# Local and pooled attention into a split-precision feed-forward: the pooled product halved over both row groups, two more units sent through DRAM, a new table of due times, and larger stores at the end

## The chip, the cores and the metric

One core of one Trainium2 chip. The time is the device time of one launch, in microseconds (us). A core has five engines with a program each: PE (matrix products, 128 x 128 cells that read weights from up to 128 partitions and can be used as smaller tiles), DVE (elementwise, reductions, 32 x 32 transposes), ACT (activations and copies), POOL (elementwise, slower) and SP (here it only issues transfers). ACT issues some transfers too. "64\*64" before a shape is the tile of PE that an instruction uses, rows by columns.

## The reference, cut to what matters

```python
# q, k, v: [8 batches, 8 heads, 576, 64]
def sm_attn(qq, kk, vv):                      # softmax(qq kk^T / 8) vv
    ...
q_d, k_d, v_d = (x.reshape(B, H, 144, 4, D).mean(axis=3) for x in (q, k, v))
out_up = np.repeat(sm_attn(q_d, k_d, v_d), 4, axis=2)      # pooled attention
mask = np.abs(pos[:, None] - pos[None, :]) < 4             # banded attention
out_local = softmax(where(mask, q k^T / 8, -1e9)) v
x = (out_up + out_local) as [4608 tokens, 512]
h = x @ w_in                                  # 512 -> 2048
g = h * np.clip(h + 3.0, 0.0, 6.0) / 6.0
out = g @ w_out                               # 2048 -> 512
```

## The kernel before, in words

**Feed-forward.** The 4608 tokens are nine chunks of 512. For each chunk and each of 16 blocks f of 128 hidden columns, `gemm1` (L1031) makes h in a PSUM bank (tiles h0, h1), ACT makes the clip (L1037), DVE the gate (L1041), ACT the rounded copy gh (L1045, `hi`), DVE or POOL the remainder gl (L1049, `lo`), and `gemm2` (L1081) adds the block into the chunk's four output banks o0 to o3. Every operand is such a pair of a rounded part and a remainder, so that each product takes three matmuls: 12 matmuls of 128 x 512 for a `gemm1`, 12 for its `gemm2`, 3456 in all. The weights are split into such pairs on the chip during the first chunk (`plan_weights`).

**Attention.** A unit is two heads of one batch: 32 units, four per batch, and chunk 0 needs the four units of batch 0, chunk 1 those of batch 1, and so on. A unit has pooled scores (a softmax over 144), banded scores (windows of 64 rows, ten of them in two halves), and two products with V. There are two kinds of units:

- *alone* (before: batches 0 and 1): each step stands by itself in PE's program. Pooled scores `scores_d` L504, mask and banded scores L699 and L707, pooled weights transposed by PE (`trans_d` L597), their product (`pv_d` L678), banded weights transposed by PE (`trans` L732), their product (`pv` L750). For V's last rows PE also does a small sum (`sum_pe` L466).
- *in bursts* (before: batches 2 to 7): weights are written to DRAM by SP (`put_d`, `put`: L610, L637), read back in another arrangement (`get_d`, `get`) and turned by DVE (`turn_d`, `turn_l`). `plan_burst` puts the scores of a new unit and the products of an older one side by side in one piece of PE's program: pooled scores (`scores_d4` L521), banded product (`pv` L750), pooled product (`pv_d4` L666), banded scores (L707). The burst holds the two banks h0 and h1 until DVE has read the results (`mean` L682 on ACT, `mean_too` L685 and `add` L755 on DVE).

In `pv_d4` the 144 pooled keys lie as three groups: group 0 on partitions 0 to 63, group 1 on 64 to 127, and group 2 (32 rows: the last 16 keys once for each of the unit's two heads) on partitions 0 to 63 with zeros filled up to 64 rows, so that products of 64 rows serve for it too.

**Order.** A planner (`Plan`) takes all operations with their dependencies, a cost each, and due times, and writes a fixed program for every engine: `start_of(n)` gives a chunk's start from `T0` and `TC`, `FIRST` the due times of batch 0, `PEN` and `COST` choose between engines for an operation that several can do. Queues are in order: an instruction that waits holds what stands behind it on its engine.

**The end.** The last chunk's output tiles are copied out of PSUM in two halves, ACT then DVE (L996, L998), and stored by SP and ACT, one transfer for each run of at most 36 rows (`stores`, L1002).

## Time and profile before

| what | value |
|---|---|
| time, median of 3 runs | 919.96 us (918.54 to 920.59) |
| the profiled execution | 915.05 us, its span 913.2 us |
| PE busy | 899.2 us, 98% of the span |
| DVE, ACT, POOL busy | 530.9, 430.1, 230.2 us |
| DMA read and written | 69.53 MB, 22.61 MB |
| chain that ended last | PE 91%, DVE 3%, DMA 2%, ACT 1% |

The profiled execution lies below all three of the timed runs (4.91 us under their median), so a sum that is made in its trace is carried to the median as a difference. In the rows of the trace a line starts with the start and the duration in us; "xN" is the count of records. Instructions on PE overlap: the next one's start minus this one's start is the time that PE spent on it. One float32 matmul on a 64-row tile leaves two records.

### The profile page before, as it was taken

How to read it: one execution, taken by the hardware profiler on the slowest of the kernel's cores; microseconds unless marked ns; L12 is line 12 of the kernel's file. 1: busy time of each engine (PE TensorE's matmuls, PEld its weight loads, DVE VectorE, ACT ScalarE, POOL GpSimd, SP SyncE). 2: the span in 40 equal slices, each digit the busy share in tenths (PEclk: the TensorE clock that was granted, in tenths of full speed). 3: DMA queues.
4: the chain of work that ended last, by engine and by line, in shares of the span. 5: the costliest groups of instructions: out<-in, count | busy, mean ns of one | idle time of the engine just before them, and what ended most of it. 6: DMA issues, size and time to landing. Idle time of an engine off the chain costs nothing.

```text
span 913.2 us, 19160 instructions
## 1 busy us (share of the span) xinstructions
PE 899.2 (98%) x7002; PEld 730.9 (80%) x7002; DVE 530.9 (58%) x965; ACT 430.1 (47%) x1438; POOL 230.2 (25%) x316
## 2 busy tenths in 40 slices
PE   8899999999999999999999999999999999999997
PEld 6577778788888888888888888888888888888886
DVE  7989866676755567556745675556654432233222
ACT  5977745566554555345535564455542222222221
POOL 5685532222322231223212330225000000010000
PEclk9999999999999999999999999999999999999999
DMA  9989433666736456355644555555522010001001
GB/s 251 290 231 293 100 82 77 128 120 134 146 85 128 100 112 144 78 104 106 139 97 93 114 116 126 105 104 105 134 59 48 1 47 1 1 1 46 1 1 46
DMA packets 311565, 93.41 MB, mean 102 GB/s; under 512 B 250800, under 2 KB 296880, under 8 KB 311472
## 3 DMA queue, kind: packets, MB, share of 16 engines
q1 hardware_dynamic: 310800, 91.29, 44.4%
q8 instruction: 55, 0.90, 0.4%
q10 hardware_dynamic: 672, 0.91, 0.3%
q14 instruction: 38, 0.31, 0.1%
HBM read 69.53 MB, written 22.61 MB: 101 GB/s over the span
## 4 chain that ended last, share of the span: by engine, by line
PE 91%; DVE 3%; DMA 2%; ACT 1%; SPq 1%; issue 1%; POOL 0%; ACTq 0%; DVEq 0%
PE h L1031 42%; PE o L1081 41%; PE a L707 2%; PE h L750 1%; PE h L666 1%; PE a L521 1%; DMA arena<-in_k_dram 1%; ACT arena L571 1%; DMA out_dram<-arena 0%; DMA pd<-arena 0%; PE a L504 0%; PE a L678 0%; SPq L985 0%; DMA arena<-in_v_dram 0%; PE a L750 0%
## 5 line engine op out<-in xcount | busy, mean ns | idle before, releaser
L1081 PE MATMUL o<-wp,rounded 128*128 128x512 f32 x1728 | 414.4, 392 | 0.0
L1031 PE MATMUL h<-rounded,wp 128*128 128x512 f32 x1728 | 407.8, 391 | 2.0 <-DVE first L755 1.4
L1031 PEld LDWEIGHTS h<-rounded,wp 128*128 128x128 f32 x1728 | 322.6, 188 | 72.0 <-issue 2.8
L1081 PEld LDWEIGHTS o<-wp,rounded 128*128 128x128 f32 x1728 | 321.2, 188 | 69.4 <-issue 0.8
L1041 DVE SCALAR_TENSOR_TENSOR arena<-arena,h 128x512 f32<-128x512 f32 x144 | 97.8, 679 | 127.1 <-ACT arena L1037 126.8
L1037 ACT ACTIVATE arena<-h 128x512 f32<-128x512 f32 x144 | 85.7, 595 | 181.7 <-PE h L1031 180.8
L1045 ACT CAST rounded<-arena 128x512 fp32r<-128x512 f32 x144 | 88.8, 617 | 112.1 <-DVE arena L1041 61.9
L1049 DVE TENSOR_TENSOR rounded<-arena,rounded 128x512 fp32r<-128x512 f32 x105 | 72.4, 692 | 101.5 <-PE o L1081 96.6
L1049 POOL TENSOR_TENSOR rounded<-arena,rounded 128x512 fp32r<-128x512 f32 x39 | 51.9, 1333 | 168.5 <-PE o L1081 88.7
L377 DVE STREAM_TRANSPOSE arena<-arena 128x576 f32<-128x576 f32 x56 | 43.3, 775 | 67.3 <-DMA arena<-in_q_dram 34.1
L571 ACT ACTIVATE arena<-arena 128x64 f32<-128x64 f32 x240 | 80.1, 336 | 0.2
L571 ACT ACTIVATION_READ_ACCUMULATOR arena<-arena 128x1 f32 x240 | 45.3, 189 | 0.0
L453 POOL TENSOR_TENSOR arena<-arena 32x256 f32<-32x256 f32 (+1 forms) x26 | 19.4, 746 | 94.4 <-DMA arena<-in_v_dram 90.7
L547 ACT ACTIVATE arena<-arena 128x1 f32<-128x1 f32 (+1 forms) x78 | 15.0, 192 | 47.6 <-DVE arena L560 47.6
L454 POOL TENSOR_TENSOR arena<-arena 32x128 f32<-32x128 f32 (+1 forms) x26 | 12.8, 494 | 96.9 <-PE h L666 95.7
L682 ACT ACTIVATE arena<-h 128x144 f32<-128x144 f32 x24 | 7.0, 290 | 63.7 <-PE h L666 63.7
L451 DVE TENSOR_REDUCE arena<-arena 128x128 f32<-128x512 f32 (+1 forms) x26 | 27.6, 1061 | 13.4 <-PE h L666 9.2
L934 POOL TENSOR_TENSOR rounded<-arena,rounded 128x768 fp32r<-128x768 f32 (+3 forms) x5 | 8.9, 1789 | 98.4 <-ACT rounded L119 94.8
L415 POOL TENSOR_TENSOR arena<-arena 128x144 f32<-128x144 f32 x52 | 31.8, 612 | 4.1
L588 DVE TENSOR_TENSOR arena<-arena 128x432 f32<-128x432 f32 (+1 forms) x42 | 29.8, 710 | 1.4
L633 DVE STREAM_TRANSPOSE arena<-arena 128x384 f32<-128x384 f32 (+1 forms) x48 | 22.2, 467 | 13.5 <-DMA arena<-pd 13.0
L707 PE MATMUL a<-arena 64*64 64x64 f32 x1160 | 28.7, 224 | 0.0
(192 smaller groups left out, 783.9 us busy)
## 6 DMA issues: line engine op xcount, KB each, us to landing
arena<-in_v_dram SPq DMA_DIRECT2D x58, 160.0 KB
rawp<-in_w_in_dram SPq DMA_DIRECT2D x16, 512.0 KB
rawp<-in_w_out_dram SPq DMA_DIRECT2D x16, 512.0 KB
arena<-in_q_dram SPq DMA_DIRECT2D x112, 72.0 KB
arena<-in_k_dram SPq DMA_DIRECT2D x112, 72.0 KB
pl<-arena SPq DMA_DIRECT2D x24, 320.0 KB
arena<-pl SPq DMA_DIRECT2D x96, 80.0 KB
arena<-in_v_dram SPq DMA_DIRECT2D x28, 256.0 KB
```

Of the source, the lines that this page charges most:

```text
L377: nc.vector.transpose(out=qk[kind], in_=qk[kind])
L415: eng.tensor_tensor(t, t, x[:, :, r], op=ALU.add)
L451: eng.tensor_reduce(out=vd, in_=raw.rearrange("p r e -> p e r"), op=ALU.add, axis=AX.X)
L571: nc.scalar.activation(x[:, j], x[:, j], AF.Exp, bias=m[:, j:j + 1], scale=0.125, accum_out=s[:, j:j + 1])
L588: eng.tensor_tensor(x, x, s.unsqueeze(2).broadcast_to(list(x.shape)), op=ALU.mult)
L707: nc.tensor.matmul(st["ps", g][half:half + WIN, jj * D:jj * D + WIN], qk_of("q")[hs, k_first:k_first + WIN], qk_of("k")[hs, k_first:k_firs ...
L1031: nc.tensor.matmul(st["ps"], win[f][:, wt, kk * P:(kk + 1) * P], xs[part][:, kk], start=(kk == 0 and i == 0), stop=(kk == NK - 1 and i == ...
L1037: nc.scalar.activation(st["t"], st["ps"], AF.Relu, bias=3.0)
L1041: nc.vector.scalar_tensor_tensor(out=t, in0=t, scalar=6.0, in1=st["ps"], op0=ALU.min, op1=ALU.mult)
L1045: nc.scalar.copy(st["gh"], st["t"])
L1049: eng.tensor_tensor(st["gl"], st["t"], st["gh"].bitcast(F32), op=ALU.subtract)
L1081: nc.tensor.matmul(otile[n, m], gt[:, ms], wout[f][:, wt], start=(f == 0 and i == 0), stop=(f == NF - 1 and i == 2),)
```

## The change

1. **Pooled product.** Group 2 is split between both row halves: its weights for the first 24 of each 48 queries stand on partitions 0 to 31, those for the other 24 on partitions 64 to 95, and its 32 rows of V on both. Four products of 64 rows by 144 columns (groups 0 and 1) are followed by four of 32 rows by 3 x 24 columns. The loads of V's last rows, `get_d`, `turn_d`, `head` and the pooled sum of V work on those places; the zeros that filled group 2 are no longer written.
2. **Kinds of units.** `ALONE, APART = 6, 8` count units: units 4 and 5 of batch 1 stay alone, units 6 and 7 go "apart": scores by themselves as an alone unit has them, weights through DRAM, both products in one piece (`pv_all`) in no burst.
3. **Due times and costs.** A table `SHIFT` gives each unit its own offset (from -22.4 to 41.8 us), `T0`, `FIRST`, `LAGW`, `KEEP`, `STAY`, `COST` and `PEN` have new values, the rounded copy gh may go to DVE ("ghi"), pairs of blocks start at block 8 of chunk 0 (`PAIR0`), and a new rule (`sooner`) lets an operation wait for another engine that would end it earlier.
4. **The end.** A tile of the last chunk is copied out by one instruction, ACT or DVE in turn, and whole runs of 36 rows go out in one transfer (`put`), in all chunks. The last two blocks' products of its first two tiles are no longer joined.

The core of the diff:

```diff
-            for g in (0, 1, 2):
-                ks = slice(g % 2 * D, (g % 2 + 1) * D)
+            for g in range(2):
+                ks = slice(g * D, (g + 1) * D)
                 for h in range(2):
                     hs = slice(h * D, (h + 1) * D)
                     nc.tensor.matmul(
-                        st["pod"][g % 2][hs]..., st["vd"][ks, g // 2, hs],
-                        used(st["pdt"][ks], h * D, 2 * D) if g < 2 else used(st["pdt"][ks], 6 * D, D),
-                        start=(g < 2), stop=(g > 0), skip_group_check=True)
+                        st["pod"][g][hs]..., st["vd"][ks, 0, hs],
+                        used(st["pdt"][ks], *((3 * h * D, D) if apart else (h * D, 2 * D))), start=True, stop=False, ...)
+            for g in range(2):
+                ks, q = slice(g * D, g * D + NAR), QB // 2
+                x = st["pdt"][ks]
+                for h in range(2):
+                    hs = slice(h * D, (h + 1) * D)
+                    nc.tensor.matmul(
+                        st["pod"][g][hs]...[:, :, g * q:(g + 1) * q], st["vd"][ks, 1, hs],
+                        bass.AP(..., ap=[x.ap[0], [D, 3], [1, q]]), start=False, stop=True, ...)
...
-            unit = plan_unit(..., due - (1 - u) * unit_time(b))
-            if b < ALONE:
+            unit = plan_unit(..., due - (1 - u) * unit_time(b) + SHIFT[NHP * b + 2 * d + u])
+            if NHP * b + 2 * d + u < APART:
...
+        elif apart:
+            a = op("PE", 1.19, pv_all, t + lv + turned_d + sums, take=bks + [ok] + xbs, ...)
...
-            def hi(st=st, key=key):
-                nc.scalar.copy(st["gh"], st["t"])
+            def hi(eng, st=st, key=key):
+                copy_on(eng, st["gh"], st["t"])
...
-            e = [op("ACT", 0.37, partial(ev_half, 0, nc.scalar), [ready], ...)]
-            e.append(op("DVE", 0.37, partial(ev_half, 1, nc.vector), [ready] + e, ...))
+            e = [op("ACT" if m % 2 == 0 else "DVE", (0.60, 0.69)[m % 2], partial(ev_last, ...), [ready], ...)]
...
-T0, TC, TF, LAG = 55.0, 82.0, 5.1, 2
+T0, TC, TF, LAG = 45.8, 82.0, 5.1, 2
-FIRST = 16.0, 8.0
-ALONE = 2
+FIRST = 4.9, 4.6
+ALONE, APART = 6, 8
+SHIFT = [
+    0.0, 0.0, 0.0, 0.0, -19.4, -16.3, -6.5, -14.0,
...
+    "ghi": {"ACT": (0.17, 1 / 1130), "DVE": (0.09, 1 / 1800)},
```

Line numbers shift with the change: `gemm1` L1031 becomes L1047, `gemm2` L1081 L1097, `pv` L750 L760, the band L707 L717, `scores_d4` L521 L522, `scores_d` L504 L505, the pooled product L666 becomes L667 (64 rows) and L676 (32 rows), the store L1002 L988.

PE's program at the first burst that holds a new and an older unit. Before, the end of the older unit's banded product (L750), its pooled product (h is the pair of banks that the burst holds), and the start of the new unit's banded scores (L707):

```order
L750 MATMUL h_2153<-arena 64x61 x2
L666 MATMUL h_2152<-arena 64x144 x2
L666 MATMUL h_2153<-arena 64x144 x2
L666 MATMUL h_2152<-arena 64x144 x2
L707 MATMUL a_2154<-arena 64x64 x2
```

The same place now:

```order
L760 MATMUL h_2157<-arena 64x61 x2
L667 MATMUL h_2156<-arena 64x144 x2
L667 MATMUL h_2157<-arena 64x144 x2
L676 MATMUL h_2156<-arena 64x3x24 x2
L676 MATMUL h_2157<-arena 64x3x24 x2
L717 MATMUL a_2158<-arena 64x64 x2
```

The third pair of products of 64 rows has become two pairs of 32 rows and half as many columns, between neighbours that use tiles of 64 rows.

PE's program in chunk 0, at unit 7, the last of batch 1. Before, its pooled and banded weights are transposed (L597, L732) and multiplied (L678) in pieces between blocks of the feed-forward:

```order
L1031 MATMUL h_1661<-rounded,wp_1376 128x512 x12
L597 MATMUL a_1688<-ident,arena 128x128 x3
L597 MATMUL a_1693<-ident,arena 16x128 x3
L1081 MATMUL o_872<-wp_1494,rounded 128x512 x3
L1081 MATMUL o_891<-wp_1494,rounded 128x512 x3
L1081 MATMUL o_899<-wp_1494,rounded 128x512 x3
L1081 MATMUL o_911<-wp_1494,rounded 128x512 x3
L678 MATMUL a_1717<-first,arena 64x144 x4
L732 MATMUL a_1723<-ident,arena 128x128 x3
L1031 MATMUL h_1731<-rounded,wp_1425 128x512 x12
L732 MATMUL a_1752<-ident,arena 128x128 x2
```

What an apart unit (here unit 6) has in their place: one piece with both products, and then blocks until the next unit's pooled scores (L505):

```order
L760 MATMUL a_1448<-arena 64x57 x2
L760 MATMUL a_1449<-arena 64x61 x2
L667 MATMUL a_1448<-arena 64x144 x2
L667 MATMUL a_1449<-arena 64x144 x2
L676 MATMUL a_1448<-arena 64x3x24 x2
L676 MATMUL a_1449<-arena 64x3x24 x2
L1097 MATMUL o_856<-wp_1355,rounded 128x512 x3
L1097 MATMUL o_870<-wp_1355,rounded 128x512 x3
L1097 MATMUL o_900<-wp_1355,rounded 128x512 x3
L1097 MATMUL o_908<-wp_1355,rounded 128x512 x3
L505 MATMUL a_1512<-arena 64x144 x6
L1047 MATMUL h_1523<-rounded,wp_1287 128x512 x12
```

The four transposing pieces of the unit are gone from PE; its weights pass SP's queue and DVE instead.

PE's program in chunk 1 between the second burst and the third (L521, the first that holds two units). Before:

```order
L1031 MATMUL h_2057<-rounded,wp_862 128x512 x12
L1081 MATMUL o_2090<-wp_726,rounded 128x512 x3
L1081 MATMUL o_1992<-wp_796,rounded 128x512 x3
L1081 MATMUL o_2003<-wp_796,rounded 128x512 x3
L1081 MATMUL o_2008<-wp_796,rounded 128x512 x3
L1081 MATMUL o_2090<-wp_796,rounded 128x512 x3
L1081 MATMUL o_1992<-wp_966,rounded 128x512 x3
L1081 MATMUL o_2003<-wp_966,rounded 128x512 x3
L1081 MATMUL o_2008<-wp_966,rounded 128x512 x3
L1081 MATMUL o_2090<-wp_966,rounded 128x512 x3
L521 MATMUL a_2154<-arena 64x144 x2
```

Now:

```order
L1097 MATMUL o_2039<-wp_805,rounded 128x512 x3
L1097 MATMUL o_1986<-wp_913,rounded 128x512 x3
L1097 MATMUL o_1991<-wp_913,rounded 128x512 x3
L1097 MATMUL o_2001<-wp_913,rounded 128x512 x3
L1097 MATMUL o_2039<-wp_913,rounded 128x512 x3
L1047 MATMUL h_2082<-rounded,wp_850 128x512 x12
L1047 MATMUL h_2112<-rounded,wp_913 128x512 x12
L1097 MATMUL o_1986<-wp_942,rounded 128x512 x3
L1097 MATMUL o_1991<-wp_942,rounded 128x512 x3
L1097 MATMUL o_2001<-wp_942,rounded 128x512 x3
L1097 MATMUL o_2039<-wp_942,rounded 128x512 x3
L522 MATMUL a_2158<-arena 64x144 x2
```

Between the two bursts stand 51 of the feed-forward's matmuls instead of 39. Behind the third burst follow 12 of `gemm2` and then a `gemm1` in both programs.

## The prediction

> **What bounds the kernel now.** I read the page first: the span, PE's busy time and the chain that ended last.

> ```profile
> span 913.2 us, 19160 instructions
> PE 899.2 (98%) x7002; PEld 730.9 (80%) x7002; DVE 530.9 (58%) x965; ACT 430.1 (47%) x1438; POOL 230.2 (25%) x316
> PE 91%; DVE 3%; DMA 2%; ACT 1%; SPq 1%; issue 1%; POOL 0%; ACTq 0%; DVEq 0%
> ```

> PE is idle for 913.2 - 899.2 = 14.0 us. Anything that is to help takes work from PE, or one of these few idle stretches. Most of the work can't move: two blocks of `gemm1` in a row show what 24 of the feed-forward's matmuls take, from the start of one group to the start of the next.

> ```profile
> 156.82 5.60 PE L1031 MATMUL h<-rounded,wp 128*128 128x512 f32 x24
> 162.26 2.20 PE L1081 MATMUL o<-wp,rounded 128*128 128x512 f32 x9
> ```

> 162.26 - 156.82 = 5.44 us, 0.2267 each; 3456 of them are 783.5 us, and no part of the change touches their number. The idle stretches are next, the largest of PE's waits inside the feed-forward and the stretch where PE is emptiest before the feed-forward runs through.

> ```profile
> PE h L1031 <- DVE first L755: 1.4, 2, 1.3
> 20.00:40.00 20.00, 17.68 (x309) 12.25 (x309) 18.85 (x49) 16.74 (x50) 16.07 (x24) 1.00 0.94 266
> ```

> In the first row (total, times, longest) a `gemm1` waited 1.3 us in one place for DVE's `add`. In the window 20 to 40 us (the columns are PE, PEld, DVE, ACT, POOL busy, the granted clock, DMA share and GB/s) DVE is busy 18.85 of 20 us: this start is DVE's, and PE is idle 2.32 us in it. The clock is 1.00, so nothing below depends on it.

> **Units 6 and 7 through DRAM.** An alone unit's price is the distance between the first rows of two units of batch 1, less the feed-forward between them.

> ```profile
> 97.45 0.39 PE L466 MATMUL a<-arena,four 64*16 64x128 f32 x2
> 97.77 0.95 PE L504 MATMUL a<-arena 64*64 64x144 f32 x12
> 98.65 3.02 PE L1081 MATMUL o<-wp,rounded 128*128 128x512 f32 x12
> 101.50 2.88 PE L1031 MATMUL h<-rounded,wp 128*128 128x512 f32 x12
> 104.23 0.45 PE L699 MATMUL a<-maskb,identb 128*128 128x320 bf16 x2
> ...
> 105.34 3.02 PE L1081 MATMUL o<-wp,rounded 128*128 128x512 f32 x12
> ...
> 122.48 0.39 PE L466 MATMUL a<-arena,four 64*16 64x128 f32 x2
> ...
> 692.82 0.81 PE L750 MATMUL h<-arena 64*64 64x60 f32 x40
> ...
> 694.04 1.21 PE L1081 MATMUL o<-wp,rounded 128*128 128x512 f32 x4
> ```

> From 97.45 to 122.48 are 25.03 us with seven blocks of 12 matmuls, 84 x 0.2267 = 19.04; the unit costs PE 5.99. An apart unit keeps the pooled scores (98.65 - 97.77 = 0.88), mask and band (105.34 - 104.23 = 1.11) and has both products in one piece, as the last units have it (694.04 - 692.82 = 1.22). Each of the three pieces interrupts the feed-forward: the 12 matmuls after the pooled scores took 101.50 - 98.65 = 2.85 against 2.72, so 0.13 each. Together 3.60: 2.39 saved per unit, **-4.8** for two. If an interruption costs twice that, it is -4.0; these are the ends. What the two units now send through SP (two stores, twelve gathers) and DVE (two to three turns each, in place of the copies out of PSUM that are dropped) lies beside PE; it is on the path only where chunk 1 waits for unit 7, which is a rival below.

> **The pooled product.** Its price in a full burst, and the prices of a round of 144 columns and of a change of tile:

> ```profile
> 195.16 0.31 PE L521 MATMUL h<-arena 64*64 64x72 f32 x8
> 195.29 0.76 PE L750 MATMUL h<-arena 64*64 64x60 f32 x40
> 195.87 0.54 PE L666 MATMUL h<-arena 64*64 64x144 f32 x9
> ...
> 196.36 0.75 PE L707 MATMUL a<-arena 64*64 64x64 f32 x36
> 197.05 1.19 PE L1081 MATMUL o<-wp,rounded 128*128 128x512 f32 x4
> ...
> 25.43 0.95 PE L504 MATMUL o<-early 64*64 64x144 f32 x12
> 26.31 0.39 PE L466 MATMUL a<-arena,four 64*16 64x128 f32 x2
> ...
> 36.66 0.86 PE L678 MATMUL a<-early 128*64 128x144 f32 x8
> 37.45 0.82 PE L504 MATMUL a<-arena 64*64 64x144 f32 x9
> ```

> Products on different quarters of the array run together, so time goes by rounds. Before, row half 0 has four rounds of 144 columns (two records for each of groups 0 and 2), row half 1 two; the piece takes 196.36 - 195.87 = 0.49 us. L504 has six rounds and ends in a change of tile, 64\*64 to 64\*16: 6r + c = 26.31 - 25.43 = 0.88. L678 has four rounds and two changes, 128\*64 to 16\*64 within it and then to 64\*64: 4r + 2c = 0.79. So r = 0.121 and c = 0.153; four rounds by this are 0.49, as measured. The new product has two rounds of 144 columns (0.24), then products of 72 columns: 195.29 - 195.16 = 0.13 for the same number of records in L521. Its tiles have 32 rows between neighbours with 64, so two changes come in, 0.31, if such a change costs what those in the rows cost. Then the piece is 0.68, +0.19; without that cost it is 0.37, -0.12. In the 22 full bursts that is +4.1 or -2.6. At four single products (two at the end, two of the apart units) a change of tile to the feed-forward follows anyway, so only one is new: +0.04 or -0.12 each. In all **+4.3**, or -3.1 at the other end. I take the first: the change from 128\*64 to 16\*64 in L678 is a change in rows as well, and it is dear. [...]

> **The wait for PSUM at 181 us.** The 1.3 us stand behind the first full burst.

> ```profile
> 176.78 3.02 PE L1081 MATMUL o<-wp,rounded 128*128 128x512 f32 x12
> ...
> 179.13 0.44 ACT L119 COPY arena<-h 64x72 f32<-64x72 f32 x2 [1.56 <-DMA pd<-arena]
> ...
> 179.59 0.31 DVE L685 SCALAR_TENSOR_TENSOR arena<-h,arena 128x144 f32<-128x144 f32 x1 [1.27 <-ACT arena L119]
> ...
> 180.48 0.81 DVE L755 TENSOR_TENSOR first<-h,arena 128x288 f32<-128x288 f32 x2
> ...
> 181.07 1.16 PE L1031 MATMUL h<-rounded,wp 128*128 128x512 f32 x4 [1.28 <-DVE first L755]
> ...
> 198.57 0.81 DVE L755 TENSOR_TENSOR first<-h,arena 128x288 f32<-128x288 f32 x2
> ...
> 199.91 0.39 PE L1031 MATMUL h<-rounded,wp 128*128 128x512 f32 x1
> ```

> ACT's copy out of the burst's bank waits 1.56 us for the store of the former unit's pooled weights, DVE's `mean_too` waits for ACT, the two adds follow, and only then is the bank free for `gemm1`. Now 51 of the feed-forward's matmuls stand between the second burst and the third in place of 39, 12 x 0.2267 = 2.7 us more for that store. The wait goes: **-1.3** (0 at the other end). What is late next is the same path without the store: behind the next burst the adds end at 199.38 and `gemm1` starts at 199.91, so it has 0.53 us to spare.

> **The end.**

> ```profile
> 906.78 1.29 PE L1081 MATMUL o<-wp,rounded 128*128 128x512 f32 x5
> 906.84 1.65 ACTq L1002 DMA_DIRECT2D out_dram<-arena  x4
> ...
> 908.61 0.38 ACT L996 ACTIVATE arena<-o 128x256 f32<-128x256 f32 x1 [1.48 <-DMA out_dram<-arena]
> 909.02 0.42 DVE L998 TENSOR_SCALAR arena<-o 128x256 f32<-128x256 f32 x1 [1.44 <-DMA out_dram<-arena]
> 909.48 0.87 ACTq L1002 DMA_DIRECT2D out_dram<-arena  x2
> ...
> L981 DVE TENSOR_SCALAR arena<-o 128x512 f32<-128x512 f32 x21 | 14.4, 688 | 6.1 <-DMA out_dram<-arena 4.3 <-PE o L1081 1.0 <-DMA pl<-arena 0.7
> ```

> PE is done at 908.07, but ACT issues transfers until 908.5, copies its half, DVE the other until 909.44, and two more issues follow until 910.35; the span ends 2.85 later. Now DVE alone copies the last tile, 0.69 from about 908.1 to 908.8, and one issue (0.87 / 2 = 0.44) on each queue follows: 909.25, and 2.85 behind it 912.1, that is -1.1. SP's last transfer now holds three runs of 36 rows in one, 216 KB for 72 KB, so I give back 0.4: **-0.7** (ends -0.2 and -1.1). The merged stores of the other chunks are behind PE's work and cost nothing; their cover is a whole chunk.

> **Due times, costs, casts.** They add nothing to PE's work. Up to 115 of the 144 rounded copies go from ACT to DVE; DVE, 58% busy, can hold them, and where it can't is a rival. The start stays bounded by DVE: at most PE's idle 2.3 us of the window above can be won, or as much lost with the longer lists on DVE; I take **0**.

> **The sum**: -4.8 + 4.3 - 1.3 - 0.7 = -2.5. The profiled execution, 915.05 us, would become 912.5; it lies 4.9 below the median of the timed runs, to which I carry the difference: 919.96 - 2.5 = **917.5 us**. With the terms' ends (0.8 + 0.5 + 1.3 + 0.5, and the start's 2.3) this case alone runs from 914.5 to 920.8.

> **The rivals.** *A tile of 32 rows costs no change against one of 64.* Then the product gives -3.1 for +4.3: -9.9, 910.1 us. For it speaks that all tiles here are 64 columns wide; against it the 128 to 16 rows above.

> *DVE frees the banks too late (slower).* Each burst but the first leaves 0.53 us. The copies to DVE may stand right in front of `mean_too` and the adds:

> ```profile
> L121 DVE CAST rounded<-arena 128x512 fp32r<-128x512 f32 x1 | 0.4, 386 | 0.0
> ```

> At 0.39 us one such copy is covered; two, 0.77, exceed the slack by 0.24, and PE waits for that at each of 22 bursts: +5.3, so 922.8 us. From a delay of 0.53 + 2.5 / 22 = 0.64 on the change loses. For it: DVE's total rises by some 45 us. Against it: the adds wait for the burst itself, and what stands before them can be worked off while it runs.

> *Unit 7 comes late for chunk 1.* Its products end about 24 matmuls and a half burst (5.4 + 1.1 us) before chunk 1's first `gemm1`; behind them follow mean, `mean_too` and two adds (0.3 + 0.3 + 0.8), the rounded copy and the remainder, which may be POOL's:

> ```profile
> L934 POOL TENSOR_TENSOR rounded<-arena,rounded 128x768 fp32r<-128x768 f32 (+3 forms) x5 | 8.9, 1789 | 98.4 <-ACT rounded L119 94.8
> ```

> With 1.8 for it and 0.7 for the copy (the cast above, 0.39, by its columns) that is 3.9 of 6.5 us. With one more such remainder ahead of it on POOL it is 5.7; it takes two ahead to wait, and then PE stands 1 us: 918.5, inside the range.

> *The reordering does less than the sum*: the wait at 181 us stays or moves to another burst, and the start is 2.3 us longer: -2.5 + 1.3 + 2.3 = +1.1, 921.1 us.

> **How the numbers follow.** A measurement can tell about 0.2% from no change here, 1.84 us: faster is below 918.1, slower above 921.8. The forecast with the change of tile paid has 0.57; since it lies only 0.6 us below that bound, I give 0.33 of it to faster, 0.22 to same and 0.02 to slower. The rival without that cost has 0.29, all faster. DVE's delay has 0.09, all slower, the weaker reordering 0.05, half of it same and half slower. Rounded: faster 0.62, same 0.25, slower 0.13. The range reaches from 909.2, a little below the second case, to 921.0; what lies outside is the lateness on DVE and a part of the second case with a shorter start.

> **What would show it.** In the changed profile: between L667's first record in a burst and L717's main group 0.68 us if the changes are paid, 0.37 if not. Two more units without the transposing rows L598 and L742, and the stretch from chunk 0's start to chunk 1's shorter by about 4.8 us. No wait of `gemm1` for L765 behind the third burst; where PE's waits list L1047 behind L765 many times, DVE's lateness is right. The last issue ends about 1.2 us behind the last matmul, not 2.3. The forecast is wrong if the start, up to the first gate, moves by more than 2.3 us either way, or if the new order opens waits of PE in chunks 0 and 1 where DVE is at 19 of 20 us.

## The result and the profile after

The changed kernel takes **999.49 us** (median of 4 runs, 997.93 to 1001.4), the kernel before 919.25 in the same comparison: ratio **1.0876**, 95% interval 1.0847 to 1.0906. Forecast were 917.5, with a range to 921.0. This is not one of the terms a little off; something the prediction had at zero costs tens of microseconds.

The page of the changed kernel, the lines that answer to those of before (the fourth is the chain that ended last, the last two are groups of instructions: busy time, mean of one, idle time before them):

```profile
span 997.8 us, 19256 instructions
PE 927.6 (93%) x7092; PEld 742.2 (74%) x7092; DVE 584.0 (59%) x1088; ACT 372.6 (37%) x1333; POOL 184.4 (18%) x227
PEclk9999998998999998999999998999899999999997
PE 22%; DMA 2%; SPq 1%; DVE 0%; ACT 0%; issue 0%; DVEq 0%
...
L1047 PE MATMUL h<-rounded,wp 128*128 128x512 f32 x1728 | 423.4, 401 | 34.4 <-DVE arena L1057 26.0
...
L1001 DVE TENSOR_SCALAR arena<-o 128x512 f32<-128x512 f32 x16 | 11.1, 692 | 52.0 <-DMA out_dram<-arena 49.7 <-PE o L1097 1.7 <-issue 0.6
```

PE is idle for 997.8 - 927.6 = 70.2 us, where it was 14.0, and busy 28.4 us longer, with only 90 records more. Most of the second comes from the third line: slices with a granted clock of 0.8 (in tenths, 8) stand where before there were none. The last line gives the first away: in all, DVE stands still for 49.7 us before it copies output tiles out of PSUM, waiting for an earlier tile's store to land.

PE's waits, as total, times, longest:

```profile
PE h L1047 <- DVE arena L1057: 26.0, 7, 6.4
PE o L1097 <- DVE arena L1001: 8.6, 4, 4.1
PE h L1047 <- DVE first L765: 5.9, 2, 2.9
PE h L522 <- DVE arena L1057: 3.6, 4, 1.8
```

Who waits for the stores (total and times), first the changed kernel's L988, then L985 of before:

```profile
DVE arena L1001: 49.7, 12
ACT arena L999: 17.9, 5
```

```profile
DVE arena L981: 4.3, 6
```

One of the places, the end of a chunk with bursts, in the timeline of the changed kernel (start, duration, what; in brackets the idle time before it and who ended it; SPq is SP issuing transfers):

```profile
370.54 8.32 PE L1047 MATMUL h<-rounded,wp 128*128 128x512 f32 x36
...
372.42 3.13 SPq L988 DMA_DIRECT2D out_dram<-arena  x4
...
375.66 6.55 SPq L373 DMA_DIRECT2D arena<-in_q_dram  x4
380.26 0.60 ACT L999 ACTIVATE arena<-o 128x512 f32<-128x512 f32 x1 [5.56 <-DMA out_dram<-arena]
...
383.42 0.60 ACT L999 ACTIVATE arena<-o 128x512 f32<-128x512 f32 x1 [1.90 <-DMA out_dram<-arena]
383.92 0.59 ACT L1053 ACTIVATE arena<-h 128x512 f32<-128x512 f32 x1
...
384.54 0.69 DVE L1057 SCALAR_TENSOR_TENSOR arena<-arena,h 128x512 f32<-128x512 f32 x1 [8.48 <-ACT arena L1053]
...
385.28 2.08 PE L1047 MATMUL h<-rounded,wp 128*128 128x512 f32 x4 [6.43 <-DVE arena L1057]
```

It is to be read from below. PE waits 6.4 us for a bank that DVE's gate frees; the gate waits for ACT's clip (L1053); and the clip stands in ACT's queue behind two copies of output tiles (L999), each of which waits for the store of a tile that went ahead of it. The stores issued from 372.4 on release the first copy at 380.3, 7.8 us later. In the run with the stores split, below, all engines have the same order; there the stores issued at this place from 356.4 on release the first copy at 359.8, 3.4 us later, and PE takes 11.3 us for the 48 matmuls of this stretch, which take 10.9 without any wait.

And behind the wait the clock falls: the window from 385 to 390 us (seventh figure 0.67) and the first 12 matmuls after the wait, 4.40 us where a row of 12 lasts 2.88 at full clock:

```profile
385.00:390.00 5.00, 4.72 (x15) 3.82 (x16) 4.10 (x9) 3.08 (x14) 0.00 (x0) 0.67 0.49 91
```

```profile
385.28 4.40 PE L1047 MATMUL h<-rounded,wp 128*128 128x512 f32 x12 [6.43 <-DVE arena L1057]
```

### The profile page after: what moved, and what is told of

Its sections match the earlier page's. It is cut to its first block, busy times and chain, and to the rows that moved or that the text cites. A ratio compares the mean times of both kernels' runs of the same rounds, so it can differ in the third digit from the quotient of the medians.

```text
span 997.8 us, 19256 instructions
## 1 busy us (share of the span) xinstructions
PE 927.6 (93%) x7092; PEld 742.2 (74%) x7092; DVE 584.0 (59%) x1088; ACT 372.6 (37%) x1333; POOL 184.4 (18%) x227
## 5 line engine op out<-in xcount | busy, mean ns | idle before, releaser
L1047 PE MATMUL h<-rounded,wp 128*128 128x512 f32 x1728 | 423.4, 401 | 34.4 <-DVE arena L1057 26.0
L1097 PE MATMUL o<-wp,rounded 128*128 128x512 f32 x1728 | 419.1, 395 | 12.6 <-DVE arena L1001 8.6
L1047 PEld LDWEIGHTS h<-rounded,wp 128*128 128x128 f32 x1728 | 333.7, 194 | 111.8 <-DVE arena L1057 30.0
L1097 PEld LDWEIGHTS o<-wp,rounded 128*128 128x128 f32 x1728 | 323.8, 190 | 85.8 <-DVE arena L1001 11.1
L1053 ACT ACTIVATE arena<-h 128x512 f32<-128x512 f32 x144 | 85.6, 594 | 316.1 <-PE h L1047 297.8
L121 DVE CAST rounded<-arena 128x512 fp32r<-128x512 f32 (+1 forms) x121 | 52.1, 433 | 39.0 <-PE o L1097 35.1
L589 POOL TENSOR_TENSOR arena<-arena 128x640 f32<-128x640 f32 (+1 forms) x28 | 32.5, 1162 | 151.0 <-DVE arena L582 151.0
L455 POOL TENSOR_TENSOR arena<-arena 96x256 f32<-96x256 f32 (+1 forms) x27 | 21.1, 780 | 210.7 <-DMA arena<-in_v_dram 165.3
L1065 POOL TENSOR_TENSOR rounded<-arena,rounded 128x512 fp32r<-128x512 f32 x27 | 36.4, 1350 | 68.0 <-PE o L1097 37.7
L1001 DVE TENSOR_SCALAR arena<-o 128x512 f32<-128x512 f32 x16 | 11.1, 692 | 52.0 <-DMA out_dram<-arena 49.7
L411 DVE TENSOR_REDUCE arena<-arena 128x144 f32<-128x576 f32 x51 | 37.5, 741 | 0.3
L119 ACT CAST rounded<-arena 128x512 fp32r<-128x512 f32 (+7 forms) x39 | 24.6, 636 | 31.4 <-DVE arena L1057 16.5
L733 DVE TENSOR_TENSOR arena<-a,mask 128x320 f32<-128x320 f32 x48 | 23.1, 481 | 13.9 <-DMA pl<-arena 13.9
L456 POOL TENSOR_TENSOR arena<-arena 96x128 f32<-96x128 f32 (+1 forms) x27 | 12.7, 472 | 82.6 <-PE h L676 80.8
```

Source lines behind the costliest of these rows:

```text
L119: nc.scalar.copy(out_, in_)
L121: eng.tensor_copy(out_, in_)
L411: eng.tensor_reduce(out=t, in_=x.rearrange("e (q r) -> e q r", r=4), op=ALU.add, axis=AX.X)
L589: eng.tensor_tensor(x, x, s.unsqueeze(2).broadcast_to(list(x.shape)), op=ALU.mult)
L1047: nc.tensor.matmul(st["ps"], win[f][:, wt, kk * P:(kk + 1) * P], xs[part][:, kk], start=(kk == 0 and i == 0), stop=(kk == NK - 1 and i == ...
L1053: nc.scalar.activation(st["t"], st["ps"], AF.Relu, bias=3.0)
```

## What the stores do

A chunk's 512 rows of output in windows without attention, chunk 7, in the kernel before and in the changed one (the last two columns are the share of the 16 DMA engines and GB/s):

```profile
826.00:833.50 7.50, 7.50 (x34) 6.20 (x34) 3.36 (x5) 1.82 (x3) 0.00 (x0) 1.00 0.49 138
```

```profile
808.60:825.80 17.20, 15.07 (x66) 12.04 (x65) 5.48 (x10) 1.67 (x3) 0.00 (x0) 1.00 0.30 62
```

The same bytes take 17.2 us for 7.5. The merged transfer of 3 x 36 rows carries three times the rows and moves them slower. The prediction asked only for a larger transfer's bytes. The theory to test (A), which nothing up to here shows, is that the outermost dimension of a transfer's patterns decides how many of the 16 DMA engines work on it, so that 3 x 36 rows go through fewer of them than 36. Its rivals are the rounded copies on DVE (B), V's new loads, which have an outermost dimension of 2 (C), and the size of the transfer as such (D).

**Stores split again.** The changed kernel, with the merging undone at the place where a transfer is issued, so that all engines' orders stay:

```diff
-        eng.dma_start(AP(..., ap=([[DM, whole]] if whole > 1 else []) + [[32 * DM, k], [1, DM]]), ob[p:p + k * whole])
+        for w in range(whole):
+            eng.dma_start(AP(offset=... + w * DM, ap=[[32 * DM, k], [1, DM]]), ob[p + w * k:p + (w + 1) * k])
```

> The changed kernel, but each run of 36 rows of the output is a transfer of its own again (3x36x512 becomes three of 36x512), in all chunks; all engines' programs are otherwise the same. Theory A (a transfer with an outermost dimension of 3 or 2 is worked off by 3 or 2 DMA engines only, so a tile's store takes 4 to 6 us, the one output buffer stays taken, and the copies out of PSUM that wait for it hold ACT and DVE): nearly all of the loss comes back, 915 to 925 us, no wait of DVE or ACT over 2 us for out_dram at the chunk ends, and the granted clock is at 1.00 behind them. Rival B (the rounded copies on DVE are what makes gates and copies out late): stays above 985. Rival C (the V loads with a leading dimension of 2 hold the queues): stays above 980.

936.14 us, ratio 1.0170 (1.0134 to 1.0205): 1.0876 - 1.0170 is 65 us of 919. B and C are out as the main cause. But the forecast of 915 to 925 is missed, and so are two of its signs: DVE still waits for stores, 18.0 us in 11 places, up to 3.7 us, and the clock is still halved behind four waits of PE. In the two profiles the span is 997.8 - 934.1 = 63.7 us shorter: PE is idle 44.9 us less, 9.6 of them behind the last matmul, and busy 18.8 us less, for the most part since it runs less at half clock. What of this came by SP's queue, where the next loads stand behind the stores (the four loads at 375.7 take 6.55 us to issue), was not measured apart.

**Before, with merging alone.**

```diff
-            for p, k, first in stores(at, P):
+            # runs of 36 rows that follow each other: ap=[[DM, whole], [32 * DM, k], [1, DM]]
```

> The kernel before, with only one thing of the change: runs of 36 rows that follow each other in a chunk's store go out in one transfer (chunks 0 to 7; the last chunk as before). Theory A: slower by 40 to 75 us (960 to 995), with copies out of PSUM waiting for out_dram. Rival B: 919 within 0.5%.

950.78 us, ratio 1.0342 (1.0295 to 1.0390): +31 us from this one edit, fewer than the 40 to 75 expected. That the order of before leaves more room around the stores is a likely reason, but no run shows it. In it the copies wait for the stores as in the changed kernel:

```profile
DVE arena L981: 31.4, 10
ACT arena L979: 18.8, 4
```

**The outermost dimension by itself.** The first version wrote 36 rows as 2 x 18:

> The kernel before, with each 36-row transfer of chunks 0 to 7 written as 2 x 18 rows: same bytes, same number of transfers, only the outermost dimension of the output's pattern is 2 in place of 36. Theory A by the outermost dimension: each such transfer runs on 2 engines, 36 rows take about 18 x 0.1 us more one after the other than now, so slower by at least 20 us. Rival D (it is the larger transfer of 144 to 216 KB that is slow, not its outermost dimension): 919 within 0.5%.

918.17 us, as before. It tells nothing: the instruction in its trace still has 36 rows in one dimension, since steps that fit together are joined on the way. So the count of rows itself was changed, each 36 into 31 and 5, and for comparison into 32 and 4:

```diff
-            ... ap=[[32 * DM, k], [1, DM]]), st_o[n, m][p:p + k])
+            for a, e in ((0, 31), (31, 36)) if k == RP else ((0, k),):
+                ... ap=[[32 * DM, e - a], [1, DM]]), st_o[n, m][p + a:p + e])
```

> The kernel before, with each 36-row store of chunks 0 to 7 as two transfers of 31 and 5 rows, for comparison with 32 and 4. If the number of engines is the largest number up to 16 that divides the outermost dimension (31: 1, 5: 5, 32: 16, 4: 4), every 31-row piece goes through one engine, and a chunk's 512 rows, of which some 390 are in such pieces, take about 390 x 0.06 to 0.1 = 23 to 39 us in place of 7.6: slower by 50 us or more, and the share of the DMA engines is about 0.06 while they run. If rows are dealt out evenly over 16 engines in any case: like 32 and 4, within 0.5%.

> The kernel before, with each 36-row store of chunks 0 to 7 as two transfers of 32 and 4 rows: as many transfers as with 31 and 5. By the rule of the divisor 16 and 4 engines: 919 to 925, the price of 85 more issues on SP's queue only.

1050.81 us and 922.47 us (one run each; the two differ by one row, in the larger transfer or in the smaller). A stretch out of a chunk's store with 31 and 5, then with 32 and 4:

```profile
950.00:970.00 20.00, 12.30 (x45) 9.26 (x45) 4.45 (x7) 2.33 (x4) 0.00 (x0) 0.80 0.13 38
```

```profile
833.70:841.00 7.30, 7.30 (x34) 6.02 (x33) 3.36 (x5) 1.82 (x3) 0.00 (x0) 1.00 0.42 99
```

A share of 0.13 for 0.42, 38 GB/s for 99, with the chunk's same bytes in the same number of transfers, each of them small. That excludes D: what counts is the number of rows, 31 or 32. In single microseconds of the first stretch (956 to 957 us) the share is 0.06, that of one engine of 16, at 25 GB/s. And late in the changed kernel's store above, where only the engines of its last 3 x 36 rows are still at work, the share is 0.19, that of three:

```profile
823.30:824.50 1.20, 1.20 (x7) 0.99 (x6) 0.00 (x1) 0.00 (x0) 0.00 (x0) 1.00 0.19 75
```

The packets show the number of engines too. A whole chunk's store, in the kernel before, in the changed one, with 31 and 5 and with 32 and 4 rows:

```profile
DMA packets 728, 1.05 MB, mean 66 GB/s; under 512 B 216, under 2 KB 216, under 8 KB 728
```

```profile
DMA packets 593, 1.07 MB, mean 45 GB/s; under 512 B 79, under 2 KB 79, under 8 KB 591
```

```profile
DMA packets 669, 1.07 MB, mean 29 GB/s; under 512 B 156, under 2 KB 156, under 8 KB 668
```

```profile
DMA packets 808, 1.05 MB, mean 58 GB/s; under 512 B 296, under 2 KB 296, under 8 KB 808
```

Each has 512 packets of 2 KB, one for each row. The number of the tiny ones follows from the transfers: take for each the largest number up to 16 that divides its outermost dimension (the 3 of 3 x 36 stands in the output's pattern, the 2 of V's loads in the source's; 12 for 36 rows, 3 for 3 x 36, 2 for 2 x 36, 1 for 31, 5 for 5, 16 for 32, 4 for 4), and the sums are 216, 79, 156 and 296, all four as measured. In the changed kernel the transfers have 24, 2 x 36, 32, 4, 3 x 36, 16, 20, 3 x 36, 3 x 36 and 20 rows: 12 + 2 + 16 + 4 + 3 + 16 + 10 + 3 + 3 + 10 = 79. The whole executions agree: over all their transfers the sums are 14256 before and 12656 in the changed kernel, and the traces hold 14257 and 12657 packets of 4 bytes. Read with the shares of 0.06 for one and 0.19 for three, a tiny packet stands for an engine that worked on a transfer. The merged store does with 79 shares what 216 did. That shows A.

## Where the rest went

With the stores split the kernel is still 1.7% slower than before.

**V's loads.** The second suspect with a small outermost dimension is the load of V's last rows, written with a leading dimension of 2 and a step of 0:

```diff
-    raw[i * D:i * D + NAR], src(v_all, ..., [[0, 2], [4 * ROW, KR], [1, 4 * ROW]])
+    raw[i * D:i * D + KR], src(v_all, ..., [[4 * ROW, KR], [1, 4 * ROW]])
+    raw[i * D + KR:i * D + NAR], src(v_all, ..., [[4 * ROW, KR], [1, 4 * ROW]])
```

> As the run before, and also V's last rows are loaded by two transfers of 16 rows per place in place of one with a leading dimension of 2. Theory A alone: the same time as the run before within 0.3%. If the two-engine V loads cost too (rival C as a second cause): 2 to 6 us faster than it. My sum of the other terms (two units, product, PSUM wait, end without merging) says 917 to 919 for both if nothing else was wrong.

930.23 us, ratio 1.0108 (1.0069 to 1.0147), some 6 us less than with the stores alone. So C is likely a second cause; the two intervals overlap by a little, so its size is uncertain. What remains are waits for DVE:

```profile
PE h L1050 <- DVE arena L1060: 7.2, 7, 2.9
PE h L1050 <- DVE first L767: 6.0, 2, 3.8
```

The longest of them in that run's timeline:

```profile
208.53 3.59 SPq L373 DMA_DIRECT2D arena<-in_k_dram  x4
...
213.99 0.78 DVE L379 STREAM_TRANSPOSE arena<-arena 128x576 f32<-128x576 f32 x1 [3.56 <-DMA arena<-in_k_dram]
...
214.69 0.27 DVE L697 SCALAR_TENSOR_TENSOR arena<-h,arena 128x144 f32<-128x144 f32 x1
...
215.53 0.81 DVE L767 TENSOR_TENSOR first<-h,arena 128x288 f32<-128x288 f32 x2
...
216.12 1.19 PE L1050 MATMUL h<-rounded,wp 128*128 128x512 f32 x2 [3.77 <-DVE first L767]
```

DVE has nothing to do for 3.6 us: a turn of k stands in its queue ahead of the adds that free the bank, and k has been issued late. This is the place that the prediction's rival named (the adds behind a burst, 0.53 us to spare), but not with its cause: a load that is late, and no copy.

**True counts.** The planner reckons with the number of transfers that a store or a V load takes on SP; the split versions had it count the merged ones.

```diff
-            whole = 1 if r or cnt - p < RP else min((cnt - p) // RP, NC - c)
+            whole = 1
-            l = op("SP", 0.5, partial(ld4, g), ..., nd=1 if alone else 1 + g)
+            l = op("SP", 0.5, partial(ld4, g), ..., nd=1 if alone else 1 + 3 * g)
```

> The changed kernel with split stores and V loads, and with the planner told of the true number of transfers of a store and of a V load (no other number changed). If the loads are late only since SP issues more transfers than the plan counts: 918 to 921. Theory E (the order that the new numbers give is too tight whatever the count): 925 to 932.

924.14 us, ratio 1.0052 (1.0029 to 1.0075), between the two forecasts: a part of the loads was late since SP had more to issue than the plan held. This is a fault of the split versions; the changed kernel issues the merged transfers that its plan counts.

**Copies back on ACT** (`ghi` on ACT alone):

> The run with true counts, with all rounded copies gh on ACT as before the change, all other numbers of the new planning kept. Rival B in its small form (the copies on DVE make gates and adds late): 3 us or more faster, 917 to 921, and fewer waits of gemm1 for L1060. If the waits come from loads that are late in DVE's queue: the same within 0.3%, or slower by waits for ACT.

926.42 us, ratio 1.0067 (1.0039 to 1.0095): no gain. B is out in its small form too.

**The parts of the old kind.** Old planning with the units apart, and old planning with all of batch 1 alone (that is the kernel before with the new product and the new end):

```diff
-T0, TC, TF, LAG = 45.8, 82.0, 5.1, 2        (and FIRST, LAGW, KEEP, STAY, COST, PEN, PAIR0, `sooner`)
+T0, TC, TF, LAG = 55.0, 82.0, 5.1, 2
-SHIFT = [0.0, 0.0, 0.0, 0.0, -19.4, ...]
+SHIFT = [0.0] * 32
```

> The changed kernel with split stores and V loads, and with all of the planner's numbers put back to those of before (T0, FIRST, LAGW, KEEP, STAY, no SHIFT, COST, PEN, no rounded copies gh on DVE, no early pairing, no rule `sooner`); what stays of the change is the new product, units 6 and 7 apart, and the end. Theory E (the rest of the loss lies in the new order: on DVE a turn or a V sum whose load is late stands in front of the gate or of the adds that PE waits for): 915 to 919, waits of gemm1 for L767 and L1060 under 2 us in all. Rival F (the apart units and the new V and weight loads make the loads late in any order): stays at 926 to 931.

> As the run before, and units 6 and 7 alone again: the kernel before with the new product, its places of V and weights, and the new end without merging. PE's program differs from before in little but the product. By the trace of the changed kernel the product takes 0.65 us in a burst for 0.49: 22 x 0.16 + 0.1 = +3.7, the end -0.2: 3.5 us slower than before (ratio 1.004). Without a price for the change of tile it would be 3 us faster. Against the run before it should be 4.8 us slower, by the saving that I forecast for two apart units.

933.09 us, ratio 1.0152 (1.0124 to 1.0179), and 921.89 us, ratio 1.0033 (1.0013 to 1.0052). The second is what the product was reckoned to cost. The first is against theory E, which had the order alone at fault, and a little above what its rival F had (926 to 931). Here PE waits for unit 7's banded weights on their way through DRAM and then for its adds.

```profile
152.08 1.35 PE L762 MATMUL a<-arena 64*64 64x60 f32 x38 [6.71 <-DVE arena L655]
157.49 0.87 PE L524 MATMUL a<-arena 64*64 64x144 f32 x6 [3.02 <-DVE arena L767]
```

In that order at most 36 of the feed-forward's matmuls (8 us) stand between its scores and its products; the new due times put 72 there (16 us). So the units need earlier due times than the old planning gives them. The new planning with all of batch 1 alone again shows what the units bring in it and what its numbers cost:

> The run with true counts, with units 6 and 7 alone again (transposed by PE), all other numbers of the new planning kept. If the saving of 2.4 us per unit is real and only hidden by other losses: 4 to 5 us slower than the run with true counts, 928 to 929. If the units' way through DRAM costs elsewhere what it saves on PE: the same within 0.2%.

928.82 us, ratio 1.0098 (1.0064 to 1.0133): 4.2 us slower than with the units apart, as forecast. But not all of it is the alone unit's price: PE is busy 907.4 us for 904.2, 3.2 more, and a wait of 2.4 us at chunk 1's start, which the new due times give the alone unit 7, is within the time too. And it is 1.0098 - 1.0033, 6.0 us slower than with the old planning. Nor do the units pay in the old planning when only batch 1's due times are earlier (with the 64-row product of the next part):

> Old planning, split stores and V loads, product on tiles of 64 rows, units 6 and 7 apart, and the due times of units 4 to 7 earlier by 8, 16, 30 and 40 us (nothing else shifted). In PE's program 72 of the feed-forward's matmuls (16 us) then stand between unit 7's banded scores and its products, as in the changed kernel, where the run with the old due times has 24 to 36. If the waits of that run were only its late scores: 9.7 us of waits and the slow clock behind them go, and it is 4 us faster than the kernel before (product alone on 64 rows: equal to before; two units -4.2): ratio 0.995 to 0.997. If the way through DRAM is what costs: 925 or more.

> As the run before with 16, 24, 40 and 40 us: unit 7's products stand 36 matmuls earlier in chunk 0. If the first part of chunk 0, where DVE is busy 19 of 20 us, has no room for this: slower than the run before by 1 to 4 us. Otherwise the same.

1.0038 (1.0025 to 1.0052) and 1.0030 (1.0011 to 1.0048), both missed. The 6.7 us wait is gone in both, others of 1.2 to 3.1 us have come, and chunk 1 starts at 153 and 154 us, where the product alone on 64 rows starts it at 149.

**The change of tile.** The second half of the product on tiles of 64 rows, in the old planning with the units apart, with the product alone, and in the changed kernel with true counts, last also with the copies on ACT:

```diff
-                ks, q = slice(g * D, g * D + NAR), QB // 2
+                ks, q = slice(g * D, (g + 1) * D), QB // 2        (V's other rows are zero)
```

> As the run with the old planning (new product, units apart, new end), but the second half of the product uses tiles of 64 rows too (the other rows of V are zero), 64x3x24 in place of 32x3x24: same columns, no change of tile. If the change of tile costs the 0.15 us twice that I took: the product takes 0.37 us in a burst in place of 0.65, 26 x 0.28 = 7 us faster than that run, and 6 us or more faster than the kernel before (911 to 914). If it costs nothing, the same time within 0.2%.

> The run with the product alone, with the second half of the product on tiles of 64 rows (64x3x24, the other rows of V zero). In a burst the piece took 0.648 us with 32-row tiles and 0.378 with 64-row ones in the runs so far. 22 x 0.27 + 2 x 0.16 = 6.3 us faster than the run with the product alone (ratio 1.003 to before), so 2.5 to 3 us faster than the kernel before: ratio 0.997, 916 where before is at 919. If the freed time on PE only turns into waits for DVE: the same as before.

> The changed kernel with split stores and V loads, true counts, and the product on tiles of 64 rows. If PE is what bounds it: 6 to 7 us faster than the run with true counts, 917 to 918, ratio 0.998 to before. If its waits behind DVE take the gain: 920 to 924.

> As the run before, with the product on tiles of 64 rows: if both theories of loss hold (change of tile 6 us, copies 3 us), 912 to 915 and the first version here that beats the kernel before; if the copies don't matter, 920 as the run with true counts and 64-row tiles.

A burst's product in the changed kernel, from L667's first row to the band's, and in the run with the product alone on 64 rows:

```profile
363.57 0.43 PE L667 MATMUL h<-arena 64*64 64x144 f32 x8
363.93 0.35 PE L676 MATMUL h<-arena 32*64 32x72 f32 x8
364.22 0.81 PE L717 MATMUL a<-arena 64*64 64x64 f32 x40
```

```profile
405.74 0.43 PE L669 MATMUL h<-arena 64*64 64x144 f32 x8
...
406.12 0.26 PE L719 MATMUL a<-arena 64*64 64x64 f32 x2
```

From L667's (L669's) first row to the band's first row are 0.65 us with tiles of 32 rows and 0.38 with 64 throughout, for the same columns. Since the last products and the first scores of the band overlap in the second case, the whole burst is the better measure. From its first row to the feed-forward's next it takes 2.18 us before, 2.385 with tiles of 32 rows and 2.065 with 64 (medians of 21 or 22 bursts at full clock). So two changes of tile cost 0.32 us, 0.16 each, and the forecast had 0.31. PE's busy time falls by as much: 904.2 to 897.5 us with true counts, 905.7 to 898.3 with the product alone. In time that is not all seen: 930.11 us (1.0124, 1.0089 to 1.0160), 917.90 (1.0002, 0.9982 to 1.0022), 920.57 (1.0009, 0.9980 to 1.0037) and 920.08 (1.0007, 0.9985 to 1.0029), each some 2.5 to 5.5 us under its counterpart by the ratios, where 6 to 7 were expected. At least in the run with the product alone a part came back as a wait: 2.0 us of PE for the gate of a block at 232 us, with a spell of half clock behind it. No version here beats the kernel before.

## Why the prediction was wrong, step by step

The ratios form a chain from the kernel before to the changed one. Each difference times 919 us, with two ratios' intervals, some 2 to 5 us each way, behind it:

| step | from the runs | us |
|---|---|---|
| new product, new end without merging | product alone | +3.0 |
| the planning's new numbers | units alone against it | +6.0 |
| units 6 and 7 apart | true counts against units alone | -4.2 |
| split transfers that the plan doesn't count (split versions only) | V split against true counts | +5.1 |
| V's load with an outermost 2 | stores split against V split | +5.7 |
| merged stores, all chunks and the end | changed kernel against stores split | +64.9 |
| together | | +80.5 |

The fourth row is no loss of the changed kernel, whose plan counts what it issues. The last three rows belong together: against split stores and V loads that are planned for, the merged ones cost 75.7 us.

- **"The merged stores of the other chunks are behind PE's work and cost nothing; their cover is a whole chunk."** This is the step that failed: put at nothing, it costs 65 us with the end. There is one output buffer (and what is free of a few others), so a chunk's four copies wait for one another's stores, and these copies stand in ACT's and DVE's queues ahead of clips and gates that PE needs at once. The cover was not a chunk but the few microseconds between two tiles, and a chunk's store takes more than twice as long, since a merged transfer uses 3 or 2 DMA engines for 12 (by the tiny packets above, and 0.19 of the engines busy for three).
- **The end, -0.7.** The size of a 216 KB transfer was given 0.4 us, the author's estimate, which no run shows. Merged, the span ends 14.9 us behind the last matmul's end (982.9), in place of 5.1: ACT's last three issues alone take 7.7 us, while the merged transfers are under way. That is 9.6 us more than with split stores, and it is part of the 65.

```profile
980.15 4.85 SPq L988 DMA_DIRECT2D out_dram<-arena  x4
...
982.93 0.69 DVE L1014 TENSOR_SCALAR arena<-o 128x512 f32<-128x512 f32 x1 [2.03 <-PE o L1097]
983.01 7.74 ACTq L988 DMA_DIRECT2D out_dram<-arena  x3
```

  With split stores in the changed kernel's order the new end takes 5.3 us, with V's loads split too 4.9; in the later runs it takes 5.7 to 6.4. So the new end with split stores is worth 0.2 us at the best and costs up to 1.2.
- **The product, +4.3.** Right in mechanism and size: a full burst is 0.207 us longer for a forecast 0.19, with the other tile 0.113 shorter for 0.12, and the run with it alone takes +3.0 us. No row of before had a tile of 32 rows; that such a tile pays for the change between rows of 64 is shown by the runs with both, at the 0.16 us for each change above.
- **The two units, -4.8.** Right in kind: 4.2 us in time, but PE is busy only 3.2 us less, below the forecast's lower end of 4.0. What it left out is the price of the due times that the way through DRAM needs.
- **Due times, costs, casts, 0.** Mis-sized: +6.0, more than the 2.3 us allowed for the start. In the run with true counts, chunk 0's first `gemm1` starts at 35.9 us for 32.9 before, and 3.2 us are lost at 49 us to a gate behind a late load. The casts bring no gain when they are put back on ACT.
- **The wait at 181 us, -1.3.** It is gone from that place, and others like it stand behind other bursts: the path with 0.53 us to spare was rightly named, the loads ahead of it weren't counted.
- **Loads at no price.** I wrote that what goes through SP lies beside PE. V's 52 loads with an outermost 2, which count with two tiny packets each in the 12656 above (as plain 32 rows they would count with 16, 728 more in all), cost some 6 us by the two runs, and in the split versions the issues that the plan didn't count another 5.1.
- **The clock.** "The clock is 1.00, so nothing below depends on it": true of before. In the changed kernel 51 us of the span up to the last matmul run at half clock. PE is busy in 44 of them. From one 128x512 matmul to the next it takes 0.427 us there for 0.227 at full clock (medians), so by an estimate from these two some 21 us of the 28.4 by which it is busy longer come from that. None of the rivals had it.

- **The range.** The ends that the sum lists come to 0.8 + 0.5 + 1.3 + 0.5 + 2.3 = 5.4 us, so this case alone would have reached 922.9, not 920.8. The measured time lies far beyond either.

## What to carry to other kernels

Before transfers are merged, look at the outermost dimension of both patterns: 36 rows were spread well, 3 x 36 and 31 rows were not, and the same bytes then took two to four times as long. A store is only hidden if its buffer isn't needed: count the buffers, and look at what stands behind the waiting copy on its engine's queue. And a wait of PE can cost more than it lasts: here 47 us more of idle time behind the first 30 us, up to the last matmul, brought some 21 us at half clock with them, not quite half again.
